# V rows of a half pass stored row first, with a newly searched order of work, in a planned two-layer kernel

## The chip, the core and the metric

The kernel runs on one core of one Trainium2 chip. The metric is device time in microseconds (us) of one execution. The engines are TensorE (PE, matrix products), VectorE (DVE), ScalarE (ACT), GpSimd (POOL) and SyncE (SP). SP and POOL issue the transfers (DMA); the transfers themselves run on 16 DMA engines. Each engine works through its own instructions in order.

## What is computed

Two layers, each an attention with a recurrent memory followed by a gated feed-forward part, on x of shape [1, 2048, 512] in bf16 (the layers use the same weights):

```python
def A(x, mem, Wq, Wk, Wv, Wo):        # 32 heads of 128, memory of 8 rows
    for s in range(64):               # segments of 32 rows
        h = concat([mem, x[s]])       # 40 rows
        q, k, v = h @ Wq, h @ Wk, h @ Wv
        p = softmax(mask(q @ k.T * scale))
        o = (p @ v) @ Wo
        mem = o[:8]                   # goes into the next segment
        out[s] = o[8:]
def B(x, w_gate, w_up, w_down):
    return (sigmoid(x @ w_gate) * (x @ w_up)) @ w_down      # 1792 wide

x = x + A(layernorm(x)); x = x + B(layernorm(x))
x = x + A(layernorm(x)); x = x + B(layernorm(x))
```

The memory rows make the 64 segments of one layer a chain. What does not depend on the memory, such as V of the x rows, can be computed ahead.

## The kernel before

**Steps.** One step (`emit_step`) does one segment of layer 0 and, six steps behind it, one segment of layer 1, so there are 70 steps; the first six and the last six have one segment alone. A step projects Q and K (L890: weights stationary, 40 or 80 columns), forms scores (L904), does the softmax on DVE and ACT (L918 to L935), transposes the probabilities (L947), multiplies by V (L973) and by Wo (L991). V of the rows that the step needs at once is made in "strips" (L815). After every four segments the feed-forward part of a block of 128 rows follows (`ffn`: L1093 gate and up, L1117 down), its weights streamed by POOL (L1085, L1086, L1111; for the last block L1040).

**V ahead of time.** V of most x rows is computed before or beside the steps and put into a scratch tensor in DRAM (`scr`, one row of 4096 values for each of 24 rows of each segment), from where each step loads its part (L859, tile `vsb`). Three routines do it. `v_pass` (matmuls at L693) takes a tile of 128 rows. `v_half` (L730) takes 64 rows: 32 are eight rows (one octet) of four segments, 32 are sixteen rows of two segments; it puts two pieces of 1024 values under each other on the 128 partitions, and its result goes out by transfers of 64 KB, 32 rows of 1024 values. `v_strip` takes 32 rows. `v_half` runs twice: once at the start of the program for block 1, and once late for the second last block of layer 1. `take_v` and `take_part` copy the normalised, transposed rows from PSUM into the tile that the matmuls read; `take_part` does the 32 columns for the sixteen rows of two segments.

**Staging at the start.** Before and during step 0 the kernel runs seven full V passes and one half pass. Their results are cast from PSUM (L1230 on ACT, L1232 on DVE) into nine staging buffers of 1024 columns, which are the tiles `wd0-2`, `wg0-2` and `wu0-2` before their use as feed-forward weights, and stored from there (L1226) by SP or POOL. A cast into a staging buffer waits until the buffer's earlier stores have landed. At the same time SP loads all of Wq, Wk, Wv and Wo (L592). Later in the program the passes use buffers `vst` and `sst`.

**Order.** Every piece of work is a `Task` with engine, duration and dependencies. `Planner.forward` lays them out in planned time, always taking the ready task that stands first in a fixed list of priorities, which the constant `SEQUENCE` holds in packed form (found by a search outside the kernel). The instructions are then emitted in order of planned start. For a store, the plan counts `nb` bytes on a modelled bus and at least `lat` ns until the buffer is free. Where the plan leaves PE idle for more than 250 ns with little work around it, `warm` puts in filler matmuls on a zero tile (`hot`, L1216), which keep PE active and compute nothing that is used. POOL's weight loads carry a wait for the matmul that the plan has last ended before them.

Of the kernel before, what the change touches and what calls it, by code (L numbers as in the profile page):

```python
# [20 lines left out]
P = 128  # L21
MEM = 8
SEG = 32
L = MEM + SEG
LW = 2 * L
XS = 24
SCOL = 24
BLK = 4
# [3 lines left out]
def fview(base, dims):  # L32
    return bass.AP(tensor=base.tensor, offset=base.offset, ap=[tuple(base.ap[0])] + [tuple(d) for d in dims])
# [20 lines left out]
;Aht@pIrb8fB#p5?Q#$k*OKvZZTq^c3OM%bV44b=*R*ZTyW=(F)eXpo=!dnjd%&eFWe?4v9B9J-6{(d-LCut;#!E)o@XKL;|1Yh}DX~>av(XnTcNY5yDmuUNDYpk)1hbP~Icf*@B%SY3<$N!PMdC+w  # L54
TzC*H?wh$B-*Ih~y~Z^1eU45ybkQ1*)!rl+2M7#!1kA=M>_00gM+A4yerPR?|M?Mj6^>>JOVW=CEf+cd3@>&Nfi0vId6NWR);FU?#N7i-E<e}?kQ5;smk7+$yR>6M$&vA+ka>GT!8=_b4-#fP#)eF7
^yFAVNqaBx;!Z*DxPH}w4u4hwLD|Xk-(55Lk^B_BDfkRj%d!v=C<*w7SG;+fg+&T)>)vE^_U=fY&kC>YwKQIya^N!=lH>FlpJ`Jr&lF|=A)fY+g;i{E@r#X;(VDk3V2MMXacuh+Y1k_asM6Wlyelal
#hat)UmCRL92k7baU(yGZ`~C!81W~7P5Erk>AYc<Vay?}YFcMj2ofpnp$(sP&YA3~nf~n+b1fFy?|Zym`QSa144a*IfxPvGj&Q1ek!IqLN$jiF41N6_7PG1D?N__fhI#wYegIrLSdO>RI&L#ADzYcB
9Qqa8r^xHgLyr2s6(Q^~qr%E_$NJ+TpJ_bc{R>AcDm>XZ4K<5#ddGdVwMU;&cRuZ|Sp~k`OZ$e|X_~sQ@384vzE1LEOy7FI`;?xf^#@MMQ)L6bC_!Zn4S4CHx9Vjn^H}pFj3R+|IJ2mzre;noNVd$S
`{%;vED%u54cw3M^F8VWNicF9{B~XUq?7A1595()pJ)9U7U(TRXvIYfie-lrSI2C)aZ1BBh3$_bQ;!I-B=8ScYh1ck&O!bB=K^(6{|r6Qx~A%7Guq$r@Iax)(DGfYMGmfWTtN`TiNx0^a_h-)zaQ;Y
Bg~_fxFI1YgW5VrkU}+v(OG0q+i!<|tAlPcRfvDusTf+wG<zAh-6L;+Y1?sI#2|g1{X&hwViH*}otG=?Uzck!7(XzcfK!b2s0y$`SNOr$pn;5(vR*N@6t6GIu9c&BiE<wNN?P(QqaXRd3M2ScK!LD`  # L60
7NE8fpYJ@UG|VxPeYSAG0la_&djDUlCG|bBoZOzAT#$(zHi(qOLpXAuXb5%<ke>jX1k1`o2(mU?ngq;3!G;hMQLm2&9MTEUYd^USvXFM#vQ$cKmjg>LrQvGCuN0;hmD;jcN{gk}oA#{rr~t7er6x;>
4TAPsm6b5FLH-g|Nf9h4giYb{D&c`|4)4`L+JTg9TM;~}=IotkUY(*Y!dPX~EqzNqLnvA&8*(y?XY|Ec+`KUE@_SSE)gkFi<&UF6JtvvpbP{*<I0G^z6$#&pA}^v95^Q4FK#<`jp&L`QSey9`{hytp
ep4|DPRnnzJfR5<$bbinu=f`jwczBNxe3uhZ<*z*5#J~4a?5s>6axJof)V}FxLuSWLQ`X$p%|GAo3ni>PtV+JzEAC$o%TiCe#d7B$K5bY%WL%|Y?`a4x@DA(YsP8dw{qC8hys!6@G=TJ3;?U)VFlx0
p<M<>KJllT(z)CRu8?`e3^R_R7%q?S32qi7rh98c7=(LFh!0=aD^hH1fNfXqg+Sja7$z4P_WGLKlHYlxk!E{x!eD5T8C@MZ?8P+s8nOs}&1S4ol`b-NnC>Xi=go6~%Yjg-4mHO!zq-ODIoX(~$HahI
@>xN0b)~I`DIDj5VKMa;CZ!v*mkbmOJ)#~W9x(W_v;<nswK`+PTq}ipg*!qKSltnE+$xw7Xt>R@wAQgZ(cg;enc1@7fR_`9(15bKuOa8wjwP|W7E?oWno808^?XT*fvZ96JauH_vO6Tmg0YAX{%<GP
x&vaN_I%f%_>nw(eGPl2kX+vA>jgyX^`O19337j8ctxfD{|+Geiw9%@3fRrZv?20mB-ZcAf?E$T01iSEPFlGkD*OepKVV{in{2e29t=mMTqiEZTBE&ID`7X6Mk+WhT~yUj_1`*B0!BsL3UYqo?S%Vq
U~wE&tp6ZiVbg<Vu#-btWwj?J)D@CYb1QP&m*#PL94pnFvBWYRVkl3T5;SG{PpgL>Y&7Ql1a;Xg%4O>TI04XhhFijc@Xaj9&%wm+O^!e2Is7ho@U?|Mv)s#Z>S-JQQ#^hP6vJ~o=FQdi%0==QiO4>}
e22-8{8_Hk?+)?_0!^US$Hin*eL}LmU1~LxfMwEBA4T-2y4BQI`Q`64rb)aYczym_%e@Wk1AuUFK%C=ysBJZCRbO!Y(YYGT<zd6Mwt&h>Ca^n2NDBRxQWx&kPPPClqibM>xRMi&j62;fUA|z^Rcv5p
F-MNEhkhZ`GG5|d;IIVWX3i~0UVC9j1JR_k)g}?mU=2&5>*Rm+{_7pfxv?)^BxJ;D;a}CKd+}lN*i{g!Cy29Nm6fs_s@A?29$S^C=sV2}7Gf8_q&p!Q-YYz<B<R6Q_L7&#1<{@t2|<x!)7#Viogyj%
#-k9m4_)fkps3Y)zWP9b))iXN6jc_5mj%JnzCGR%<`NT61>o}26adbxHKRWL;eGC_dPO$_0O%g3i&ylcjeO4Kp62wN^0l#G6AFX@sZ^p&lw_s>8|c<!RV%n$fDjRZ^Xo3)dI6V@-wLB+#PD@hFC|K{  # L70
hmxDVz+rV(-EotTD{>}bC$E+{l9$s&EXe`8-@_@{(5~Q9mF~S=mCXo-n@iGREv|B+hO}uaWNVIcBn--!6`yjXIwzk;tw$!|KNqC$<@Mh~wq+c2tXd(#Sr5!A-C=djQjW|zR>pY8ZsJpuHW?k&Vb2JQ
uK|mZtO+LXNgAg_(QsnAn`7TMhXkU87ogepo>y~+Q6YK~1|}aZxCTk*_)GF*LQIhh36&7b>}*Sf3aF_c%*8+#IpW86KlVU=PpvHDgCV0ph`o{zROB--HMhg)Z{yqq7Md>tmspIb4I7+>36}snbBa~p
2aq{FMm-sS@IOYq2mBa3IjrPDLfH_wb!L?PC1T|kd4ugY$iW8dl9Wn@+q#mR|8AO(pY8)gqHT0JZH)K^N=vOt<7^u-*$(l~x1U$PlUtaJALTr+N%)sKo=X09?|my^)5C^3SE4k&!$P)9kk;k6_2g=+
Xo<ZissDeGX{x7oi<<eTlp~=irUE^K35dz<U*p)9mm+d=#S6VL#4*xk?AUu>i@32H9Xk7!kk_K%&o5%^Sg@sug$7E7OfE13qWWUI<gX~Ww=Ovk<b`gMnA(LF)GbK-eGV(1eZq-0q2A1%j71R50jC+4
(YzP{LgPu!joT@AK^rRGm+vVYvgOLUd8rkU;M*n6fXUc#<4{U(<*Jw%^s|AolsW{O5e?q{R_5NdEk8h+662I+)Aqfs4y9uUn};G(N@<LuFs|^cT2FPBk6;o7V$@9XgP@*E$knBwHr>Rl>{fn#3`Kt?
yh8LxMxizaxtE9ijw|3QBSBOL8_*nr`Ija$bn=z6WE8x*$~+<;`&N15!cf9T9fLAG-W%WU!ZwOoz+`YmAGo$BFvfAhCU$wVm+!7~hqUD?_Qj=5pJZxrj>B%sT+T>^Mpe?7D7;6#U{20sx38&r-oZv<
@f;0J3*rnK+>gY7iHrU98Tc!cU$yG52J(53IMpe}CyZMp-M}xnkjatQP^<S=pQKx;v4)WilNu5`<Za2;cEYv!A-^%SNfLQcZHw<TrO#PTqr1ut(uD2lWlxw84HtnVFYJyK21!>3Pf#x4_<auBIOT|n
+@;+PE;I~5c;iLu7VSwLd!<@@giENcHgyQSL;-J2%c`n1>tw)5Bs}veFA<rH!^3m=l`VY}Nszs5V--R@?57p?P(+>mj+CH3TAIxks-M;?YeONKMhQ_kw+?5>kTJHu|7yVyF>aFUs;2k$08rksLjZ&}
Rec5D4v+VLqz!LXr1aXx264-a^;D{bA9Zt}4bb>Bb_oPv)r^`d2*V&n2Ps(kqh|OKVk6^jP`eI67p;O+<c~o`+;F|9sQaL-_ZCgX_3J6psL~YuH;xzf`)FU$t#f-U$eq7GKrs6{7FHkpW}34-RKFM*
9&x(UP}Ft7D%r_qN6h*20^EO0T}Wm?E1yp5ENr4Ju^T6EzeEMp)Bxm$T|rJ-CxTow#WGfD?k-in)T%Z8GRC)%u=eaRl_Ei`LMbFvL;YDLA~vt~$m$JHk6jxGBe&YFI+>Nh?*OuRiCPnCt@Nm2(HxK7  # L80
#&3kRM`t_Q;5~4|e>TMT4t<3*yUdt-xWMmna~NN*hW^#KJ3(n?D%%4`{Q+jJuR0q4-_lBy1j+FBqmip{O6sP`{bVE4hNzX|>QS_7B!LY(zVBx%^%(gHKijzO7Ss7Y(G2Y2VQ+E`6%mA5j&X?^I+)=|
P<db;>vgq@xzey}P_~g3{N0R$zl8UO=BM~MHCS_OrtXQ46onh0Y#OYaL!ZE2hoY+*G}tq}KBV|{#L!ZpbzLAaT=ge(F?IDIVMCq|mJBTHQ7CK5JO9=<=;)u%Yj;dLVc$R@gieZ`3AQh;6$rQ@iQZ@=
V>RB0haCzv329qrPHxI7KHybS8kD}@tey_pdZ+S3^+1!Zd_u(#@Bwc51(75!RI^zH@e*z62rR(bpoRk@rSm4S)S>3R3(Wmz*PCj{K$|na6?y2wU-w!(O%p6C9;oB8ZWV&<g-`Z^=HY<$y{^Z}jzCH3
UV$HD&VAwr6NtQ=vm`Xi+b-%FeG1g-5T&0ujXOTbNIQ{--zb|ZXytJtlj%7Tc{m1gKrfa#1X|V|As@F`7PH^zsG86&KLMk?>yZwc_JoAGr4WCLyeG~q5GD-oSX}2SSUvbPtzotDQV0E)5@I+Lha>C&
DS}ZGSn^mAJ`rlJm$5wePawoBajMO_l>j@?a2^U6_XSpq6S=J&H%kq4yvh*XzCIoZEU5NZczw6pMsmG}ABT=!bK@{MoQf~)lh)A0R22|G2BZt657mYk*_Tox-<g_09hV%;nL)YWonN|3AoDDx&1bL#
na*q83IB<G*_XVk%zy^teDZs~klOgm%HrUN2`M2h$pxj`RxaLf?mzW9jL{u4b|2D$NCMsLEnv^EJh#UKVL&G@cccOKTX~vm=xXk>U(k{q><I@&qD4ep%cxk8wmbLK%on{EPuT3?KiL3BsfB_s1}bzk
4k|w0K9P#^uUS|!0xaU$hu;r;-r3W&(`9`69^o6k9MDHHCCOPN>8OGEB7kEu=OXx}z3lSM@#1-PR{12eGz$@r>xDR@OeAgi{t+wvo>a0$WAP0PR9xFiZje_>iXPbTL!I&>UXu+LdY@e1wZR>E17rZB
_+1n?x+n@BHD(xyH5M3>DojQSVA(+cjxuKoi`As`(3r341mYa=<Gnp#T0tV^_cl4vhHpPKWj~AM*68j?JL({AjU)?K8UBd2%9vf(4s6E?TZ5#2(31QOu_voI?SmO95M~gstN^S&ygMVMa+7$!j~~*w
>n0u^sTKie_itwQlu@d`$Zj>onhtI!b0vvzI)BHLoRI$U?9LZM)w3v7pp8=Wpl7T(#6V4<Yi}9FIZDO+1savChV`Bwh!a{l%y(g|5;5s7w^124BDWWQHs3LPqOE<c0yvy1C^1zPbcI>H>xn!)3D3@R
0ejF8VuC8mkDGEa&ISH)g{aX_*WmOWBZF4(w=N*V^Q|3g%A^g5GeDl>1C_i%H2H#=*lDDJa2^QLXVdUf&jgBJXyA@u?p3@x%H%c$e0#Fu<fvQcuJ;TBqCnx9iYc^$QG7^^dbn&AkGoUyANwJZSqPhK  # L90
Ac>4^b;;ty(xTHUj2Jk&pY&#O3PT@VMEmFVd&dixCF6K<_$liKg3Cj*V%4jhO3@Wv#1C|H^oLjrm!TiSpn57#u77vrsh{=&Bkb^MTE8UmD`d-2n0-lFoX^MDTotFvOL_g{o`^VVLKK*p6%^F6_vHwy
L%E;$n_9PyS)iahe;p1n{}jFulI{!Q1ducj@Bbp282b;W9E58@b2ydomxZm{=_sh)pl*hMxqO1J>PY^+m4UKxeO8+f+8jLgrYvd@;1y27j3(5TF_=J=u{nd(<XyYI*}vjdwexVPNW<`~(nxQV`Q3bm
?-oKCugIcU$CVRPsibT<&C{`K8rw`m={?5dMI#P67pVd5XXX!^kt#O7jdXHtpC<=aQ_M-IF1c$;XZ^`K2CoLbmqR$Ivq{#PQJlH<ka(UMG@!Wy?g!OE;NF9YA=d6(hACy`S2&ca19}PpzuBXTH08Tu
@Lz?f1zQpJ>%+nhM7NU7yh@DH3;cUaFfmvXqEpg)AVAQFNWD5-cvZBj8C+?m#N=#2Gz`(7O!lBeMK#0m|1R1c7XDoN+Wi~qW$PQ}4iTimXzlVCmsLkEz@waJu_xEIADt!`c|AG5*imf6#OId*7Omc%
qaSm5>$72OwOoYELPh^-&@7Cs=@8jZsTMRf!amf|sTUxf>V*{4CGsTvibsUK&XTPA+hHsZ3PI1D<FlDN+@A@t933*jJ1!OX*s2Pp$90mq4+}v0yg#t*hCdVr+krL5Y2j14j40Fk8#jZ7N*okytgprx
RoHXPQ>sp|qSDHq>3xvdg;+6VhrdRa&E_m8?%9AM0TPy1JQMu{){ovpB9COdT^_c<EN`3f$n$c_`mRbTrd}lj^xn?M>P}XdptxnwQf0TIqV&^G9k3bqu^`cP>6-h=l3S1LvjFU*kOXblPG4e&Z--0E
+KhA|kTn<6k|h`R`SZ$l@Oss%2G~13Q-M0VSk1Z`OA9`BGJ=fH_Oc3Xv<Fj}eMi@iZ>m!MW2RF5Y@NbA;&M@_i@z@lO}~Tk2qmy$XZgEXy*xS3zgC_1$wK@jWjKs|ETZb2|0cV;KeBM8Uew32FhHk<
g2?JK%8cPAmwQ$OY6r?+a;<v(-M7Hlwh@ahq}H<85-$X?@JSbXE2?g5?(sr-a(*h{<wT>lJ=Q#V6#SmiIfE3+i=WW-Uc3Bi+M*W2C~08AQAXzaep+y0(7sVh)!;#B2t36^j}s4`QIIT`gP<(b<y}U;
# [361 lines left out]
class Kern:  # L460
# [222 lines left out]
    def v_pass(self, tile, keys, pieces, boot=False):  # L683

        nc, pl, DC = self.nc, self.pl, self.DC
        w = 2 if boot else 1
# [609 lines left out]
```

## Time and profile before

| | us |
|---|---|
| median of 4 runs | 1788.21 |
| lowest, highest run | 1786.0, 1788.65 |
| the profiled execution | 1786.84 |
| span of the profiled execution | 1785.1 |
| PE busy in it | 1755.4 |
| DVE, ACT, POOL busy | 1142.9, 1164.7, 575.4 |
| filler matmuls (L1216) | 103 pieces |

The span runs from the first to the last instruction of the profile; the profiled execution's own time is 1.7 us more. Matmuls are pipelined: a PE row of the timeline gives the start of its first and the modelled end of its last matmul, so neighbouring rows overlap by about 0.17 us. The mean granted clock of PE is 0.999 of full speed. The waits in the profile are inferred from semaphores; a wait for several things is put down to the one that came last.

### The profile page before, as it was taken

Reading aid. Unit: us, or ns where it says so; the run is one execution under the profiler, and the core shown is the slowest. Engines: PE = TensorE matmul, PEld = TensorE weight load, DVE = VectorE, ACT = ScalarE, POOL = GpSimd, SP = SyncE. Lnnn points to the kernel's source line nnn. Section 1 sums busy time; section 2 is a strip of 40 time slices with the busy share of each in tenths; the row PEclk is TensorE's granted clock in tenths of the full one; section 3 lists DMA queues with packets and bytes.
Section 4 is the critical chain, followed back from the end, with each engine's and each line's share of the span. In section 5 each row is a group of like instructions: output and inputs, shape, how many; then the busy total and the mean of one; then the engine's idle time right before and its main releaser. Section 6 shows DMA issues by size and latency. Waiting matters only on the chain.

```text
span 1785.1 us, 91985 instructions
## 1 busy us (share of the span) xinstructions
PE 1755.4 (98%) x39870; PEld 1518.1 (85%) x40077; DVE 1142.9 (64%) x3944; ACT 1164.7 (65%) x2960; POOL 575.4 (32%) x827
## 2 busy tenths in 40 slices
PE   9999999999999999999999999999999999999998
PEld 4588888988898898889888898988888888989886
DVE  4366566776667567656666676657656765666665
ACT  5666656666666667666766666666666666667564
POOL 4314031413333242323324231333324232333332
PEclk9999999999999999999999999999999999999999
DMA  9825254635555464455546453555555354555543
GB/s 320 278 77 150 74 154 121 182 106 153 162 156 155 135 175 124 137 150 165 158 127 202 133 154 106 161 161 165 157 148 171 110 146 139 158 155 147 157 142 94
DMA packets 138599, 270.66 MB, mean 152 GB/s; under 512 B 32954, under 2 KB 71746, under 8 KB 138194
## 3 DMA queue, kind: packets, MB, share of 16 engines
q0 software_dynamic: 56624, 181.91, 34.6%
q1 hardware_dynamic: 81570, 82.86, 16.4%
q8 instruction: 314, 5.14, 1.2%
q14 instruction: 91, 0.75, 0.1%
HBM read 220.41 MB, written 25.69 MB: 138 GB/s over the span
## 4 chain that ended last, share of the span: by engine, by line
PE 89%; DVE 5%; issue 2%; ACT 1%; DMA 1%; POOL 1%; SPq 0%; ACTq 0%; DVEq 0%; POOLq 0%
PE bank L890 31%; PE bank L991 16%; PE bank L1093 10%; PE bank L693 8%; PE bank L815 7%; PE bank L973 4%; PE bank L904 4%; PE bank L1117 4%; PE bank L947 2%; DVE st L918 1%; PE bank L1216 1%; PE bank L662 1%; DMA wg<-in_B_w_gate_dram 1%; DVE small L930 1%; DVE st L925 1%
## 5 line engine op out<-in xcount | busy, mean ns | idle before, releaser
L890 PE MATMUL bank<-hT,wk_sb 128*128 128x80 bf16 (+1 forms) x8960 | 621.6, 198 | 1.2 <-issue 1.2
L890 PE MATMUL bank<-hT,wq_sb 128*128 128x80 bf16 (+1 forms) x8960 | 622.0, 198 | 0.6
L1230 ACT CAST qku<-bank 128x480 bf16<-128x480 f32 (+3 forms) x770 | 387.9, 512 | 221.4 <-PE bank L890 139.5
L890 PEld LDWEIGHTS <-wq_sb 128*128 128x128 bf16 x8960 | 454.4, 99 | 34.1 <-issue 23.3
L890 PEld LDWEIGHTS <-wk_sb 128*128 128x128 bf16 x8960 | 450.7, 99 | 1.4 <-issue 1.4
L918 DVE TENSOR_TENSOR st<-bank,cst 40x240 f32<-40x240 f32 (+3 forms) x768 | 278.3, 368 | 188.3 <-PE bank L904 180.0
L991 PE MATMUL bank<-otsb,wo_sb 128*128 128x80 bf16 (+1 forms) x8960 | 363.6, 198 | 1.8 <-ACT otsb L1230 0.4
L991 PEld LDWEIGHTS <-wo_sb 128*128 128x128 bf16 x8960 | 336.8, 99 | 16.3 <-issue 2.0
L1086 POOL DMA_DIRECT2D wu<-in_B_w_up_dram x217 | 164.4, 758 | 241.2 <-PE bank L1093 96.5
L1230 ACT CAST otsb<-bank 128x480 bf16<-128x480 f32 (+3 forms) x420 | 199.6, 482 | 64.7 <-PE bank L973 51.7
L1085 POOL DMA_DIRECT2D wg<-in_B_w_gate_dram x217 | 164.4, 758 | 236.5 <-PE bank L1093 93.3
L1111 POOL DMA_DIRECT2D wd<-in_B_w_down_dram x217 | 154.2, 711 | 221.7 <-PE bank L904 90.6
L928 ACT ACTIVATE st<-st 80x240 f32<-80x240 f32 (+3 forms) x420 | 159.3, 381 | 37.2 <-DVE st L925 35.0
L652 POOL TENSOR_TENSOR small<-small,cst 128x1 f32<-128x1 f32 (+1 forms) x80 | 45.2, 566 | 426.8 <-DVE small L651 426.4
L1093 PE MATMUL bank<-xnT,wg 128*128 128x128 bf16 (+2 forms) x1784 | 171.5, 218 | 1.4 <-DMA wg<-in_B_w_gate_dram 0.5
L1093 PE MATMUL bank<-xnT,wu 128*128 128x128 bf16 (+2 forms) x1784 | 171.0, 218 | 0.0
L930 DVE TENSOR_REDUCE small<-st 80x6 f32<-80x240 f32 (+3 forms) x420 | 150.9, 361 | 19.5 <-ACT st L928 16.9
L904 PE MATMUL bank<-qku 128*128 128x80 bf16 (+1 forms) x2240 | 160.1, 198 | 2.0 <-DVE pb L935 0.6
L925 DVE TENSOR_TENSOR st<-st,small 80x240 f32<-80x240 f32 (+3 forms) x420 | 154.5, 369 | 3.1
L935 DVE TENSOR_TENSOR pb<-st,small 80x240 bf16<-80x240 f32 (+3 forms) x420 | 153.8, 369 | 4.0
L923 DVE TENSOR_REDUCE small<-st 80x6 f32<-80x240 f32 (+3 forms) x420 | 151.6, 362 | 4.1
L973 PE MATMUL bank<-ptsb,vsb 104*128 104x80 bf16 x2048 | 139.3, 199 | 1.8 <-ACT ptsb L1230 0.2
(103 smaller groups left out, 2343.6 us busy)
## 6 DMA issues: line engine op xcount, KB each, us to landing
wg<-in_B_w_gate_dram POOLq DMA_DIRECT2D x220, 256.0 KB, 4.3
wu<-in_B_w_up_dram POOLq DMA_DIRECT2D x220, 256.0 KB, 4.3
wd<-in_B_w_down_dram POOLq DMA_DIRECT2D x220, 256.0 KB, 4.3
vsb<-scr SPq DMA_DIRECT2D x460, 48.0 KB
vsb<-sst SPq DMA_DIRECT2D x464, 32.0 KB
scr<-vst SPq DMA_DIRECT2D x112, 96.0 KB
wv_sb<-in_A_Wv_dram SPq DMA_DIRECT2D x8, 512.0 KB
wq_sb<-in_A_Wq_dram SPq DMA_DIRECT2D x10, 384.0 KB
```

What stands on the lines that cost most here:

```text
L890: nc.tensor.matmul(o_ap, lhsT=W[:, c, h * P:(h + 1) * P], rhs=mv(c), start=(c == 0), stop=(c == DC - 1))
L904: nc.tensor.matmul(s_all(SB)[:, w0 + i, :], lhsT=fview(qku[:, i, 0, 0:1], [(1, P)]), rhs=qku[:, i, 1, 0:ncol], start=True, stop=True)
L918: pl.add("DVE", dve_ns(n, True), lambda gsz=gsz, hs=hs, st=st, SB=SB, pj_=pj_, npj_=npj_, mk=mk, idx=idx: nc.vector.tensor_tensor(out=st[p ...
L925: pl.add("DVE", dve_ns(n), lambda gsz=gsz, hs=hs, st=st, mx=mx: nc.vector.tensor_tensor(out=st[pr, hs], in0=st[pr, hs], in1=mx[pr, hs].uns ...
L928: pl.add("ACT", act_ns(n), lambda hs=hs, st=st: nc.scalar.activation(out=st[pr, hs], in_=st[pr, hs], func=ACTF.Exp, scale=self.scale), r=s ...
L930: pl.add("DVE", dve_ns(n), lambda hs=hs, st=st, sm=sm: nc.vector.tensor_reduce(out=sm[pr, hs], in_=st[pr, hs], axis=AX.X, op=ALU.add), r=s ...
L973: nc.tensor.matmul(fview(OB[:, o:o + 1], [(ncol, 2), (1, L)]), lhsT=self.vsb[halves[u // 8]][0:64 + L, j, (u % 8) * P:(u % 8 + 1) * P], rh ...
L991: nc.tensor.matmul(WB[:, c * ncol:(c + 1) * ncol], lhsT=self.wo[:, h, c * P:(c + 1) * P], rhs=otsb[:, hl, 0:ncol], start=(h == 0 and c == ...
L1085: pl.add("POOL", 760, lambda wg=wg, fs=fs: nc.gpsimd.dma_start(out=wg[:], in_=self.wgv[:, :, fs]), r=[("wo", self.H - 1)], w=[gk] + bt, la ...
L1086: pl.add("POOL", 760, lambda wu=wu, fs=fs: nc.gpsimd.dma_start(out=wu[:], in_=self.wuv[:, :, fs]), r=[("wo", self.H - 1)], w=[uk] + bt, la ...
L1093: nc.tensor.matmul(gu[:, 2 * i + k, 0:n], lhsT=W[:, c, i * P:(i + 1) * P], rhs=xnT[:, c, rw], start=(c == 0), stop=(c == DC - 1))
L1230: nc.scalar.copy(out=dst, in_=src)
```

## The change

Three things change together.

1. In `v_half`, the 32 rows that are sixteen rows of two segments are laid out and stored with the row first and the segment second; before, the segment came first. The outer dimension of the transfer's DRAM side goes from 2 to 16. `take_part` writes its columns in the new order. There are eight such transfers in the program, four at the start and four late.
2. The plan's figures: a store at the start holds its buffer for 5.0 us in place of 4.5 (`lat`), and the 64 KB stores of `v_half` and `v_strip` count 80,000 bytes in place of 65,536 (`nb`).
3. `SEQUENCE` is another list (104 packed lines, all different).

```diff
 SEQUENCE = r"""
-;Aht@pIrb8fB#p5?Q#$k*OKvZZTq^c3OM%bV44b=*R*ZTyW=(F)eXpo=!dnjd%&eFWe?4v9B9J-6{(d-LCut;#!E)o@XKL;|1Yh}DX~>av(XnTcNY5yDmuUNDYpk)1hbP~Icf*@B%SY3<$N!PMdC+w
...
 """
@@ v_pass
-                       lambda vs=vs, d=d, c0=c0, n=n: ("dma", d, vs[c0:c0 + BLK * n, 0:512 * w]), lat=3000.0 + 1500.0 * boot,
+                       lambda vs=vs, d=d, c0=c0, n=n: ("dma", d, vs[c0:c0 + BLK * n, 0:512 * w]), lat=3000.0 + 2000.0 * boot,
@@ take_part
-        dst = fview(tile[:, 0, c0:c0 + 1], [(P, self.DC), (n, 2), (1, n)])
+        dst = fview(tile[:, 0, c0:c0 + 1], [(P, self.DC), (1, 2), (2, n)])
@@ v_half
-                                     (32, d.rearrange("(i r) e -> i r e", i=BLK)[i16:i16 + 2, r16:r16 + 16], (r16 // 8, r16 // 8 + 1))):
+                                     (32, d.rearrange("(i r) e -> r i e", i=BLK)[r16:r16 + 16, i16:i16 + 2], (r16 // 8, r16 // 8 + 1))):
-                           lambda lo=lo, i=i, dd=dd, flat=flat: ("dma", dd, flat()[64 * i + lo:64 * i + lo + 32, :]), lat=3000.0 + 1500.0 * boot,
-                           r=[(sb, 0), (sb, 1)] + (["boot"] if boot else []), use=[sb], nb=65536,
+                           lambda lo=lo, i=i, dd=dd, flat=flat: ("dma", dd, flat()[64 * i + lo:64 * i + lo + 32, :]), lat=3000.0 + 2000.0 * boot,
+                           r=[(sb, 0), (sb, 1)] + (["boot"] if boot else []), use=[sb], nb=80000,
@@ v_strip
-                        r=[(sb, 0), (sb, 1)], w=[("vd", j, b, q8, kk) for kk in (2 * i, 2 * i + 1)], lat=3000.0, use=[sb], nb=65536)
+                        r=[(sb, 0), (sb, 1)], w=[("vd", j, b, q8, kk) for kk in (2 * i, 2 * i + 1)], lat=3000.0, use=[sb], nb=80000)
```

What the built programs show of it: apart from filler, both have the same matmuls, and the filler goes from 46,976 to 49,920 columns. PE's order differs in the first 170 us, in places between about 400 and 670, 760 and 940, and 1380 and 1740 us of the profile of before, and in the last step; elsewhere it is the same. At the start the stores are dealt anew between POOL and SP and among the nine buffers, and SP issues the x rows and the weights in another order. Some twenty copies in all change between ACT and DVE.

## The prediction on record

> **What bounds the kernel now.** I read the engine shares first, then PE's busy time in short stretches, then the chain of waits where PE stood still. One line of the page carries the first step:
>
> ```profile
> PE 1755.4 (98%) x39870; PEld 1518.1 (85%) x40077; DVE 1142.9 (64%) x3944; ACT 1164.7 (65%) x2960; POOL 575.4 (32%) x827
> ```
>
> The span is 1785.1 us and PE is idle for 29.7 us of it. PE's instruction stream is fixed except for its filler matmuls (L1216), so the time is real work + filler + idle + whatever runs at a reduced clock. A change of order can only move the last three. The 50 us stretches give where the idle lies: 1.3 in 0 to 50, 3.5 in 50 to 100, then 0.2 to 1.9 in each up to 1750, and 4.1 in the last 6 us, behind the last matmuls. Only 50 to 100 has one large piece. In steps of 2 us (columns: length, PE, PEld, DVE, ACT, POOL busy, clock, DMA share, GB/s):
>
> ```profile
> 56.00:58.00 2.00, 2.00 (x11) 0.94 (x10) 0.00 (x0) 0.00 (x0) 0.00 (x0) 1.00 1.01 356
> 58.00:60.00 2.00, 0.32 (x2) 0.04 (x1) 0.00 (x0) 0.00 (x0) 0.00 (x0) 1.00 1.02 326
> 60.00:62.00 2.00, 0.57 (x3) 0.29 (x3) 0.00 (x0) 1.20 (x3) 0.00 (x0) 1.00 1.06 344
> 62.00:64.00 2.00, 2.00 (x8) 0.73 (x6) 0.00 (x0) 2.00 (x5) 1.46 (x3) 0.59 1.03 335
> 64.00:66.00 2.00, 2.00 (x7) 0.76 (x6) 0.00 (x0) 0.94 (x3) 0.71 (x2) 0.55 1.08 345
> 66.00:68.00 2.00, 2.00 (x32) 0.81 (x34) 0.00 (x0) 1.28 (x3) 0.30 (x1) 1.00 1.07 387
> ```
>
> PE stops for 3.1 us, every compute engine with it, and for the next 4 us its granted clock is 0.55 to 0.59. PE's timeline prices the slow part, against a normal run of the same matmul:
>
> ```profile
> 43.97 4.48 PE L693 MATMUL bank<-wv_sb,xvf 128*128 128x512 bf16 x20
> 61.43 5.30 PE L693 MATMUL bank<-wv_sb,xvf 128*128 128x512 bf16 x16 [3.11 <-ACT wu L1230]
> ```
>
> The chain that ended last, and the waits in the first 100 us, name the cause:
>
> ```profile
> 52.23 0.64 SPq L1226
> 52.87 0.05 issue
> 52.92 1.63 SPq L592
> ...
> 54.65 6.04 DMA scr<-wu
> ...
> 60.80 0.59 ACT wu L1230
> 61.39 0.04 issue
> 61.43 5.30 PE bank L693 x16
> ```
>
> The wait itself (us in total, times, longest):
>
> ```profile
> ACT wu L1230 <- DMA scr<-wu: 10.6, 2, 7.0
> ```
>
> A cast into staging buffer wu (third of its ring) waits 7.0 us for the buffer's last store, which stood on SP's queue behind a weight load whose issue alone took 1.63 us; ACT is in order, so PE runs out of PSUM banks. The other wait in that 10.6 (3.6 us) cost PE nothing.
>
> **The change part by part.** The 20 matmuls from 43.97 need (4.48-0.17)/20 = 0.216 us each, where 0.17 is the overlap of the last one with what follows; the 16 after the stop should take 16 x 0.216 + 0.17 = 3.63 and took 5.30. So the stop costs 3.11 + 1.67 = **4.78 us**.
>
> *The staging reuse.* I added up the matmuls in both built orders (0.216 per 512 columns, 0.025 per 40) to place every cast and store. Before, the two tight reuses of that buffer leave 3.99 and 4.17 us of PE work between its last cast and the next; the second one has one store on POOL and one on SP. After, they leave 3.89 and 4.63, and both stores of each stand on POOL; every buffer with a store on SP is now refilled 9.7 us of work later or more. The first reuse is like the first of before, which did not stop PE. For the second: work position 46.76 was at 50.40 us on the clock in before, 3.64 later; so the last cast (position 45.78) runs at 49.4 to 50.0 and POOL issues the two stores at about 50.0 and 50.6 (0.55 each). POOL's stores landed 4.7 to 7.2 us after issue between 17 and 53 us when the queues were full (3.3 in one lull): 55.3 to 57.8. PE has work up to position 54.33 (two banks of step 0's projections, a transpose and three V banks stand behind the blocked cast, against four V banks before), about 58.1 us; a landing needs 0.7 more for the cast. The stop becomes 0 to 0.4 us: take off **4.78**.
>
> The skill's page "TensorE: Matmul & The Clock Gate" (Part 1, What's actually happening) has the clock fall after an idle window of about 3.4 us. The row shows 0.55 after 3.11 us. By the page the stop would be worth 3.1, by the row 4.8; the row decides.
>
> *Row first, segment second.* Eight stores of 64 KB change from 2x16 to 16x2 rows of 2 KB. In before the four on POOL landed in 6.1 to 7.2 us, 8x4 stores of the same size near them in 4.7 to 7.0: about 0.8 us later. But their buffers are refilled 14 us of work later, and what they write is first read in step 4; the four near the end (1598 to 1608 us) have no waiter in the trace. The copy that lays the rows out now writes every second element: one on ACT, 0.27 us for the like copy, with 0.36 us of idle behind it. I take 0; bounds -0.4 (one 0.4 us wait at the late staging buffer) and +0.2 (the copy doubling without cover).
>
> The page "DMA: Bandwidth & Descriptors" (Why a DMA increments its semaphore by 16 and not by 1) picks the largest number of engines up to 16 that divides both slowest dims, so 2 becomes 16. Another section (Issuing engines are not separate DMA queues) speaks against a gain: all queues share the 16 engines. With DMA shares of 1.01 to 1.08 in the stretches above, the one rule would bring these stores forward, the other moves no byte earlier; no run shows the new form yet.
>
> *Start of the program.* SP issues the x rows and V weights in another order, POOL puts two more memsets (0.23 each) ahead of its first small op. The filler up to the first V matmul goes from 23,936 to 23,808 columns: -0.05 us. POOL's first small ops at 6.91 and 9.09 have 1.4 us idle between them, which hides the memsets.
>
> *Steps 1 to 3.* Four V matmuls move from step 1 into step 0, and filler grows by 1,408 columns, 0.6 us. PE idles 1.05 us in 100 to 150, which the filler may replace: -0.46 to +0.6; I take **+0.5**.
>
> *Last step.* The same work between its V strips and its last transposes, with 1,536 more filler columns: 0.65 us. PE had 0.35 us of idle there (1750 to 1770), so +0.3 to +0.65; I take **+0.5**. After the transposes the chain goes by layernorm and is the same; POOL's last loads are released by the same places.
>
> ```profile
> 1750.00:1760.00 10.00, 10.00 (x328) 8.52 (x321) 6.40 (x21) 6.40 (x20) 2.06 (x4) 1.00 0.18 45
> 1760.00:1770.00 10.00, 9.65 (x229) 8.15 (x227) 6.44 (x28) 5.82 (x22) 5.25 (x7) 1.00 0.70 200
> ```
>
> *What is late next.* With PE 4.8 us earlier, Wo (first used at 80.5, where the weight load waited 0.4 us for it) is next. DMA shares of 0.94, 0.55, 0.86, 0.77, 0.75, 0.55 from 68 to 80 leave 3.2 us of free DMA time to bring its bytes forward; up to 1.6 us may be lost. SP's own hold there (73.8 to 77.2) is for a cast that moves along. I take **+0.3**.
>
> *Middle.* From about 400 to 670, 760 to 940 and 1380 to 1740 us the order differs in places, with equal work and filler. The 50 us stretches they fall in (400 to 650, 750 to 950, 1400 to 1700) have 8.0 us of PE idle; a tenth either way is 0.8. I take 0.
>
> Sum: -4.78 - 0.05 + 0.5 + 0.5 + 0.3 = **-3.5 us**. The profiled execution took 1786.84 (span 1785.1 and 1.7 around it), giving 1783.3; it lies 1.4 below the median of the runs shown, 1788.21, and I forecast against that: **1784.7**.
>
> **The rivals.** *A stop stays (1788 to 1790):* a store lands later than 7.2 us, or Q and K weights, asked for 4.8 us sooner, do; PE stops for up to 3 us again. For it: full DMA queues to 68 us. Against: the margin above, -0.4 to 2.1 us (58.1 - 0.7 - landing), and SP was waiting for casts at 66.2 to 69.2. The 4.8 goes back and +1.2 of filler and the like stays: 1789.4 at the worst.
>
> *Slower by over 0.2%:* the first reuse (position 35.7) becomes a stop too. It has 0.1 us less work than before, where ACT already waited 3.6 us; a store 1.5 us later than before, from POOL's denser row of issues, starts PE's idle, and from 3 us of it the clock falls. Its place is near 40 us, its price 3.1 + 1.67; with the second stop also kept, +4.8 + 1.2 = +6.0: 1794.
>
> *The order is better than counted:* stop gone, filler covering idle (-0.46 in steps 1 to 3), middle -0.8, no Wo loss: -4.78 - 0.05 - 0.46 + 0.3 - 0.8 = -5.8: 1782.4.
>
> *It doesn't do what it says:* the wider stores shorten nothing anybody waits for. That is part of the forecast; it costs no time.
>
> **How the numbers follow.** Forecast (1783 to 1786.6) 0.62; a stop stays 0.16; slower 0.13; better 0.09. About 0.2%, 3.6 us, is what a measurement of this kernel can tell from no change: the border is 1784.6, inside the forecast's case, which I split 0.35 faster, 0.27 same. Faster 0.44, same 0.43 (0.27 + 0.16), slower 0.13. The range reaches from 1782.0, the best case with the 0.4 us of the staging buffer, to 1789.5, the stop kept in full; it leaves out the slower case.
>
> **What would show it.** Right: no PE idle over 1 us and no clock below 0.9 between 20 and 100 us; the casts into wu wait under 4 us each; the strips of step 0 start near 62 instead of 66.7; Wo waits under 1.6 us; the last step 0.3 to 0.65 us longer. Wrong: a stop with a clock near 0.55 anywhere before 80 us, or matmuls of L890 or L991 waiting for weights.

## The result and the profile after

The changed kernel takes 1789.31 us (median of 35 runs, 1785.81 to 1792.69), the kernel before 1787.87 (54 runs, 1784.43 to 1790.67): a ratio of 1.001 with a 95% interval of 1.0005 to 1.0015. So it is 0.9 to 2.7 us slower, where 3.5 us less was forecast. The profiled execution took 1788.3, its span is 1786.5, 1.4 more than before.

The engine shares of the page say nothing of a loss: PE's busy time is what it was (1755.6 for 1755.4).

```profile
PE 1755.6 (98%) x39874; PEld 1517.4 (85%) x40085; DVE 1146.4 (64%) x3943; ACT 1166.3 (65%) x2961; POOL 573.7 (32%) x828
```

PE's idle time and clock by stretches of 2 us (columns as in the prediction; the last three are clock, DMA share, GB/s) show two places:

```profile
42.00:44.00 2.00, 1.14 (x7) 0.43 (x5) 0.00 (x0) 0.67 (x2) 0.00 (x0) 1.00 1.10 358
44.00:46.00 2.00, 1.90 (x11) 0.94 (x12) 0.00 (x0) 2.00 (x5) 0.33 (x1) 1.00 0.28 93
46.00:48.00 2.00, 1.95 (x10) 0.94 (x10) 0.77 (x2) 2.00 (x5) 1.98 (x5) 1.00 0.53 164
48.00:50.00 2.00, 2.00 (x14) 1.01 (x13) 0.41 (x1) 1.79 (x4) 2.00 (x5) 1.00 0.72 180
...
60.00:62.00 2.00, 0.23 (x1) 0.10 (x1) 0.00 (x0) 0.87 (x3) 0.00 (x0) 0.98 1.04 310
62.00:64.00 2.00, 2.00 (x6) 0.76 (x5) 0.00 (x0) 2.00 (x5) 0.49 (x1) 0.50 1.02 337
64.00:66.00 2.00, 2.00 (x7) 0.75 (x6) 0.00 (x0) 0.79 (x2) 0.58 (x2) 0.67 1.10 351
```

The stop at 60 us that was to go is there, with the slow clock behind it. The earlier place is new: PE misses 0.86 us at 43 us, and right behind it the DMA share, which was 1.10, falls to 0.28. The transfers have run dry, between stretches with shares of 1.10 (42 to 44 us) and 1.09 (50 to 52 us). PE's timeline gives the length of both stops and who ended them, the list of waits (0 to 110 us) the casts behind them:

```profile
43.97 0.38 PE L662 MATMUL bank<-cst,xn 128*128 128x128 bf16 x4 [0.86 <-ACT wu L1230]
...
61.77 5.30 PE L693 MATMUL bank<-wv_sb,xvf 128*128 128x512 bf16 x16 [2.03 <-ACT wu L1230]
```

```profile
ACT wu L1230 <- DMA scr<-wu: 12.2, 2, 6.2
```

Before, that line read 10.6 and 7.0. Both casts wait, as before, for stores of the buffer that they refill. The chain that ended last names the store of the second one:

```profile
50.97 0.59 ACT wu L1230
51.57 0.28 issue
51.85 0.54 POOL scr L1226
52.38 8.64 DMA scr<-wu
61.13 0.59 ACT wu L1230
61.77 5.30 PE bank L693 x16
```

It was issued at 52.4, not at 50.6, and took 8.64 us, not 4.7 to 7.2. Why the transfers ran dry is on SP's timeline:

```profile
36.56 3.01 SPq L592 DMA_DIRECT2D wk_sb<-in_A_Wk_dram  x2
45.41 0.56 SPq L1226 DMA_DIRECT2D scr<-wd  x1
46.01 1.37 SPq L754 DMA_DIRECT2D scr<-sst  x2
47.43 0.44 SPq L592 DMA_DIRECT2D wk_sb<-in_A_Wk_dram  x1
47.91 1.30 SPq L754 DMA_DIRECT2D scr<-sst  x2
49.26 0.45 SPq L592 DMA_DIRECT2D wk_sb<-in_A_Wk_dram  x1
```

From 39.6 to 45.4 us SP issues nothing. It stands at a store of wd, whose cast stands on ACT behind the cast that waits for wu. Four stores of `sst` that were ready (their casts ran at 33.3 to 34.7) and the next weight loads stand behind it. Before, SP stood only from 42.1 to 44.2, and the DMA share fell less:

```profile
41.71 0.35 SPq L777 DMA_DIRECT2D oxT<-in_A_x_dram  x1
44.24 0.64 SPq L1226 DMA_DIRECT2D scr<-wd  x1
```

```profile
44.00:46.00 2.00, 2.00 (x13) 0.94 (x11) 0.41 (x1) 2.00 (x6) 1.50 (x3) 1.00 0.73 241
46.00:48.00 2.00, 2.00 (x11) 0.89 (x10) 0.69 (x1) 1.63 (x4) 2.00 (x5) 1.00 0.87 284
48.00:50.00 2.00, 1.95 (x38) 1.46 (x37) 0.58 (x2) 1.15 (x3) 1.76 (x4) 1.00 0.73 158
```

POOL, which issues most of the stores here, stands behind the same casts on ACT, for 6.94 us after the change and 5.43 before. The row of after and then that of before:

```profile
45.67 0.52 POOL L1226 DMA_DIRECT2D scr<-wd  x1 [6.94 <-ACT wd L1230]
```

```profile
44.51 0.54 POOL L1226 DMA_DIRECT2D scr<-wd  x1 [5.43 <-ACT wd L1230]
```

Where the 1.4 us of span arise, by the start of the same matmuls in both profiles:

| place | before | after | difference |
|---|---|---|---|
| first V matmul (L693) | 13.55 | 13.43 | -0.12 |
| strips of step 0 (L815) | 66.66 | 67.00 | +0.34 |
| transposes of the first feed-forward part (L1061) | 138.70 | 140.52 | +1.82 |
| the same, ahead of the last step | 1748.94 | 1750.58 | +1.64 |
| last transposes (L1061) | 1769.41 | 1770.90 | +1.49 |

All of it lies in the first 140 us, most of it behind the strips of step 0; the last step gave 0.15 back. In the last step PE is busy throughout, as the windows that answer to those of before show:

```profile
1750.00:1760.00 10.00, 10.00 (x328) 8.37 (x324) 5.09 (x16) 5.18 (x14) 1.13 (x2) 1.00 0.12 30
1760.00:1770.00 10.00, 10.00 (x245) 8.35 (x243) 7.50 (x31) 7.00 (x27) 5.39 (x8) 1.00 0.67 191
```

### The profile page after: what moved, and what is told of

Same layout as the page of the kernel before. It is cut to its first block, busy times and chain, and to the rows that moved or that the text cites. A ratio compares the mean times of both kernels' runs of the same rounds, so it can differ in the third digit from the quotient of the medians.

```text
span 1786.5 us, 92001 instructions
## 1 busy us (share of the span) xinstructions
PE 1755.6 (98%) x39874; PEld 1517.4 (85%) x40085; DVE 1146.4 (64%) x3943; ACT 1166.3 (65%) x2961; POOL 573.7 (32%) x828
## 3 DMA queue, kind: packets, MB, share of 16 engines
q0 software_dynamic: 56256, 181.98, 34.7%
## 4 chain that ended last, share of the span: by engine, by line
PE 89%; DVE 5%; DMA 2%; issue 2%; ACT 1%; SPq 1%; POOL 0%; POOLq 0%; DVEq 0%; ACTq 0%
PE bank L890 31%; PE bank L991 16%; PE bank L1093 10%; PE bank L815 7%; PE bank L693 7%; PE bank L904 4%; PE bank L973 4%; PE bank L1117 4%; PE bank L947 2%; DVE st L918 1%; PE bank L662 1%; DVE small L930 1%; DMA wv_sb<-in_A_Wv_dram 1%; DVE small L923 1%; DVE st L925 1%
```

## The experiments

**The theory.** The two tight refills are not two separate stops. The first cast that waits (up to 43 us) holds ACT; SP, in order, holds at a store whose cast stands behind it on ACT; the transfers run dry; the loads and stores that follow are late, and PE pays later, at the second refill or at weights. The rivals: each wait costs what PE stands at it and no more; the row-first form is slow; the new order costs something elsewhere. The plan's figures (part 2 of the change) act only through the order and were not run apart.

The columns of the table: each ratio is to executions of the kernel before that ran beside the variant. "Free DMA" is 2 us x (1 - DMA share) added over the four windows from 44 to 52 us, nothing for shares over 1. "Stops" are PE's idle pieces over 0.5 us between 20 and 100 us, with what ended them ("at Wo's matmuls" where the profile names no transfer). The last column is the time from the first V matmul to the strips of step 0 (without a stop in it, 48.41 in the new order and 48.15 in the old).

| kernel | ratio (95% interval) | free DMA | stops | V to strips |
|---|---|---|---|---|
| before | 1 | 1.34 | 3.11 cast | 53.11 |
| after | 1.0010 (1.0005 to 1.0015) | 2.94 | 0.86 cast, 2.03 cast, 0.57 at Wo's matmuls | 53.57 |
| e1 after, old rows | 1.0006 (0.9997 to 1.0016) | 1.92 | 1.11 cast, 0.57 and 1.47 Wk | 49.82 |
| e2 after, both waits gone | 0.9976 (0.9966 to 0.9986) | 0.00 | 0.97 at Wo's matmuls | 48.41 |
| e3 after, first wait gone | 0.9977 (0.9969 to 0.9986) | 0.18 | none | 48.41 |
| e4 after, second wait gone | 1.0010 (1.0002 to 1.0019) | 2.48 | 0.64 cast, 2.83 and 2.05 Wk, 1.25 at Wo's matmuls | 49.46 |
| e5 before, new rows | 1.0006 (0.9997 to 1.0015) | 1.72 | 2.90 cast | 51.22 |
| e6 before, both waits gone | 0.9975 (0.9966 to 0.9983) | 0.20 | 0.81 Wo | 48.15 |
| e7 after, one store to POOL | 0.9995 (0.9986 to 1.0004) | 1.92 | 1.80 cast, 0.83 softmax, 1.09 Wo | 50.63 |
| e8 e3 without filler | 0.9990 (0.9981 to 0.9998) | 0.08 | 1.50 Wo | 48.41 |
| e9 after, plan's rule altered | 0.9978 (0.9967 to 0.9989) | 0.00 | 1.52 Wo | 48.41 |
| e12 before, first wait gone | 0.9975 (0.9965 to 0.9984) | 0.04 | 1.74 cast, 1.40 Wo | 50.06 |

The exchanged buffers are one line in `run` behind the plan; k is a task, the number behind it the staging buffer that its pass gets (0 to 2 wd, 3 to 5 wg, 6 to 8 wu). The instructions and their places stay.

**e1_old_rows**

```diff
-        dst = fview(tile[:, 0, c0:c0 + 1], [(P, self.DC), (1, 2), (2, n)])
+        dst = fview(tile[:, 0, c0:c0 + 1], [(P, self.DC), (n, 2), (1, n)])
-    (32, d.rearrange("(i r) e -> r i e", i=BLK)[r16:r16 + 16, i16:i16 + 2], ...
+    (32, d.rearrange("(i r) e -> i r e", i=BLK)[i16:i16 + 2, r16:r16 + 16], ...
```

> The changed kernel with the 16 x 2 rows laid out and stored segment first again; the order of all instructions stays. My theory (the time is lost at staging buffers that are refilled before their stores have landed, whatever the form of the rows): within 1 us of the changed kernel, PE stops at about 43 and 60 us stay within 0.5 us of 0.86 and 2.03. Rival (the row-first form itself is slower to land and costs the gain): 2 to 5 us faster than the changed kernel, and the stop at 60 us gone. Rival in the other sense (the form brings a gain that the order eats up): 1 to 4 us slower.

Measured: 1788.12 us; the interval of the ratio overlaps with that of the changed kernel, so the form is no measurable part of the loss. The second half of the expectation missed: in the one profile PE does not stop at 43 us and stops 1.11 instead of 2.03 at 60 us, but then 0.57 and 1.47 us at Wk. What the buffers gave, the weights took: PE is idle for 4.9 us between 20 and 100 us, for 4.7 in the profile after.

**e2_both_buffers, e3_first_only, e4_second_only**

```diff
         order = self.pl.plan()
+        [setattr(next(bf for bf in self.pl.bufs if bf.pool is self.bootp and k in bf.users), 'slot', s) for k, s in moves]
```

with `moves` of e2 ((211, 6), (191, 8), (282, 2), (292, 3), (318, 5), (330, 7), (324, 8), (312, 6)), of e3 ((211, 6), (191, 8), (282, 6), (312, 8), (361, 6)), of e4 ((282, 2), (292, 3), (318, 5), (330, 7), (324, 6), (312, 8)).

> The changed kernel with staging buffers exchanged between eight passes, so that the two casts that wait for a buffer's stores get buffers whose stores landed long before; every instruction keeps its engine and its place. My theory: both stops of PE go, 0.86 + 2.03 + 1.67 = 4.6 us less than the changed kernel, some 1784.7 against the 1789.3 of its median, less 0 to 1 us that weights of Q, K and Wo may take back. Rival (the weights, not the buffers, are the bound of this stretch): the stops come back at matmuls that wait for weights, gain under 2 us.

> The changed kernel with only the first of the two waits taken away (the cast at 43 us goes into another buffer; two buffers change places from there on, so that the later cast still waits for the same two stores). Theory of the chain (ACT's first wait holds SP behind a store, the DMA queues run dry from 44 to 49 us, loads and casts come late, and so the second stop): the DMA share from 44 to 48 us rises from 0.28 and 0.53 to over 0.8, and the second stop shrinks under 0.5 us; 3.5 to 5 us less than the changed kernel. Rival (each wait by itself: the second stores land late since the queues are full whatever came before): the second stop stays at 1.5 to 3 us and the gain is 0.5 to 1.2 us.

> The changed kernel with only the second wait taken away (the cast at 61 us and those after it get buffers in the order in which these come free; the cast at 43 us waits as before). Both theories: the stop of 2.03 us at 60 us and the slow clock behind it (1.67) go, 3.7 us less than the changed kernel at most. Theory of the chain: loads are late from the dry stretch at 44 to 48 us, so part of it, 0.5 to 1.5 us, comes back as waits for Q, K or Wo weights before 90 us. Rival (each wait by itself): 3.2 to 3.9 us less.

Measured: e2 1783.2, e3 1783.53, e4 1788.4 us, beside 1787.48 of the kernel before. e3 is the experiment that decides. It leaves the second cast waiting for the same two stores, and the second stop is gone all the same; with a ratio of 0.9977 it is 0.33% under the changed kernel (1.0010), 5.9 us. "Each wait by itself" promised 0.5 to 1.2. Its windows, where the changed kernel has shares of 0.28, 0.53 and 0.72, and the wait that is left:

```profile
44.00:46.00 2.00, 1.95 (x13) 1.05 (x13) 0.41 (x1) 1.17 (x2) 1.50 (x3) 1.00 1.09 381
46.00:48.00 2.00, 2.00 (x10) 0.91 (x10) 0.36 (x1) 1.27 (x3) 0.13 (x1) 1.00 1.10 388
48.00:50.00 2.00, 2.00 (x14) 1.01 (x12) 0.41 (x1) 1.27 (x3) 1.29 (x3) 1.00 1.02 370
```

```profile
ACT wu L1230 <- DMA scr<-wu: 3.3, 1, 3.3
```

3.5 to 5 us less was expected. The cast now waits 3.3 us instead of 6, which cost PE nothing; the two stores that it waits for landed 6.1 and 6.0 us after issue instead of 8.6 both. e4 is the counterpart: the second stop is gone too, and nothing is won, for PE then waits for Wk, in PE's timeline:

```profile
72.38 0.27 PE L890 MATMUL bank<-hT,wk_sb 128*128 128x40 bf16 x4 [2.83 <-DMA wk_sb<-in_A_Wk_dram]
74.80 0.31 PE L890 MATMUL bank<-hT,wk_sb 128*128 128x40 bf16 x4 [2.05 <-DMA wk_sb<-in_A_Wk_dram]
```

I had expected 0.5 to 1.5 us of that; it was 4.9 at Wk and 1.25 at Wo's matmuls. In the changed kernel the same matmuls start at 72.56 and 72.76 us without a wait, so up to there the second stop had hidden weights that were late as well. Why the second Wk transfer lands later still in e4 is not shown.

**e7_store_on_pool** takes SP's hold away and leaves the first wait; task 183 is the store of wd that SP issued at 45.4 us:

```diff
         order = self.pl.plan()
+        [setattr(tk, 'on', 'POOL') for tk in order if tk.idx == 183]
```

> The changed kernel with one store (of a third buffer, 16 x 4 rows) moved from SP to POOL: it is the one that SP waited with from 39.6 to 45.4 us. The cast at 43 us waits as before. If SP's hold is the link between the first wait and the second stop: the DMA share from 44 to 48 us rises from 0.28 and 0.53 to over 0.8, the waits for Wo weights before 90 us go, and the time falls by 2 us or more though PE's stop of 0.9 us at 43 us stays; the second stop falls under 1 us. Rival (the late casts are the link: their stores come 1 us late into full queues): the DMA share rises but the second stop stays at 2 us or grows, and the time changes by less than 1.5 us.

Measured: 1787.83 us, 0.15% (2.7 us) under the changed kernel by the two ratios, whose intervals just fail to meet, with the first stop even longer (1.80). SP issues stores and loads from 39.9 on; the share is 1.06 at 44 to 46 and 0.85 at 46 to 48, and PE does not stop at 60 us. So SP's hold is a link of the chain, worth about 2.7 of the 5.9 us. It is not all of it: SP then stands at its next store, from 44.8 to 50.8, POOL stands 7.87 us at a store of wd, the share falls to 0.47 and 0.72 at 48 to 52, and Wo is 1.09 us late, which I had expected to go. No run takes away POOL's hold alone, so how the other 3.2 us divide is not shown.

```profile
44.00:46.00 2.00, 0.93 (x7) 0.55 (x7) 0.00 (x0) 1.67 (x4) 0.00 (x0) 1.00 1.06 361
46.00:48.00 2.00, 1.95 (x10) 0.88 (x9) 0.00 (x0) 2.00 (x5) 1.31 (x3) 1.00 0.85 291
48.00:50.00 2.00, 2.00 (x14) 1.01 (x13) 0.68 (x2) 2.00 (x5) 2.00 (x5) 1.00 0.47 156
```

**e9_plan_rule** asks why the plan lets this happen, though the change raised its hold time of a staging buffer to 5.0 us:

```diff
-            T[bf.users[0]].acq.append(bf)
+            for u in bf.users[:1] if len(bf.pool.tiles) != 9 else [u for u in set(bf.users) if T[u].eng == ("PE",)]: T[u].acq.append(bf)
...
-                need.setdefault(id(bf.pool), []).append(bf)
+                if bf.slot is None: need.setdefault(id(bf.pool), []).append(bf)
...
-                for bf in tk.acq:
+                for bf in [bf for bf in tk.acq if bf.slot is None]:
```

> The changed kernel with one rule of its planner altered: a staging buffer is taken when the first of its two halves is laid out, whichever half that is (in the kernel as it stands it is taken at the lower-numbered half, so a pass whose upper half runs first writes into a buffer that the plan counts as taken later). The priorities stay; PE, DVE and SP keep their instructions' places, the buffers' names change, and the plan's 5.0 us now hold for every refill. If the refill of a buffer in flight is the whole cause: no cast waits over 1 us for a store, no stop of PE, DMA share over 0.8 from 44 to 48 us, and 1783.5 to 1785 where the kernel before has 1787.5 to 1789, a ratio of 0.9965 to 0.9985. Rival (something else in the new start costs as well): 0.999 or more, with waits for Q, K or Wo weights.

Measured: 1784.11 us, 0.9978; no cast waits for a store over 1 us, no stop until Wo (1.52). A pass fills its buffer in two halves. The plan takes the buffer at the half with the lower number (L261); where the priorities run the upper half first, its cast is planned into a buffer that the plan has not yet taken, and no hold time guards it. Both tight refills are of that kind, before and after. With the rule mended, the new priorities alone give what e3 gives.

**e5_rows_alone, e6_before_buffers, e12_before_first** do the same to the kernel before. The diff of e5 is that of e1 the other way round, on the kernel before; e6 and e12 have the line of e2 with other moves:

```diff
+        # e6:  moves = ((180, 4), (203, 8), (282, 2), (300, 3), (318, 6), (292, 1), (330, 8), (324, 5), (312, 4))
+        # e12: moves = ((180, 4), (203, 8), (282, 4), (324, 8))
```

> The kernel before with the row-first form alone (copy and store), its own order and figures. My theory: nobody waits for these stores soon, so no difference that can be measured, a ratio of 0.9993 to 1.0007 to the kernel before, and its stop of 3.1 us at 58 us stays within 1 us. Rival (16 rows let more engines take part, and the transfer lands sooner): the four stores on POOL land under 5 us instead of 6.1 to 7.2, and the time falls by 1 us or more.

> The kernel before, its order and its form, with staging buffers exchanged so that its two casts that wait (3.6 and 7.0 us) get buffers that are long free. My theory (the refill of a buffer whose stores are in flight costs the time, not the rest of the order): the stop of 3.11 us and the slow clock behind it (1.67) go, and the time falls by 3.5 to 4.8 us, to the level of the changed kernel with its first wait taken away (1783.5), within 1 us. Rival (the new order itself is the better one): it stays 1.5 us or more above that level, through weights that come late or a stop elsewhere. Rival in the other sense (the new order costs 1 us through its added filler): 1 to 1.5 us below that level.

> The kernel before with only the first of its two waits taken away (3.6 us at 42 us, which cost PE nothing; two buffers change places from there on, and the later cast still waits for the same two stores, one of them on SP behind a weight load). Theory of the chain: also here the first wait, through SP's hold (42.1 to 44.2 us) and the dry stretch behind it, makes much of the second stop; the stop of 3.1 us falls under 1.5 and the time by 2 to 4.8 us, with a DMA share from 44 to 50 us of over 0.9 in place of 0.73 to 0.92. Rival (in this kernel the second stop has its own cause, the store on SP behind the load): a stop of 2.5 us or more stays, and the time changes by less than 1 us.

Measured: e5 1789.75 us, no difference that can be measured, yet its rival had half of it right: the four 16-row stores on POOL landed 5.1, 5.2, 5.6 and 5.5 us after issue (under 5 was expected), 6.4, 6.1, 7.2 and 6.7 before. Three stores of the same size in 8 x 4 rows among them, whose form did not change, took 5.5, 5.8 and 5.5 for 5.6, 5.7 and 6.2. The row-first form lands sooner, and nobody waits for it. e6 took 1784.5 us, 0.9975: the old order without its waits is as good as the new one without them (0.9977), so neither order is better, and neither rival held. e12 took 1783.45 us, 0.9975. The wait that cost PE nothing in the profile before was worth the whole 4 us in the times; the stop in its one profile fell from 3.11 only to 1.74, between the two theories, and Wo is 1.40 late in it. That profile is of one of its two slowest executions (1786.0 us; the median is 1783.45).

```profile
60.18 3.61 PE L693 MATMUL bank<-wv_sb,xvf 128*128 128x512 bf16 x16 [1.74 <-ACT wg L1230]
```

**e8_no_filler**

```diff
-            fill = self.pl.warm(order)
+            fill = {k: v for k, v in self.pl.warm(order).items() if self.pl.tasks[k].start < 20000.0}
```

> The changed kernel with its first wait taken away, and without the filler matmuls behind the first 20 us (16.7 us of PE time by the trace). As I priced filler (1.0 of 1.25 us is paid): 10 to 13 us less, if the clock holds. If filler stands where PE would wait anyway: no gain, and the same time or up to 3 us more where the clock falls in the gaps; PE's idle time grows by what the filler took.

Measured: 1786.47 us, 0.9990 where e3 has 0.9977. The kernel without this filler is 0.13% (2.3 us) slower. (The 16.7 us of the expectation add up trace rows that overlap; at 0.216 us for 512 columns the 26,112 columns of filler behind the first V matmul are 11.0 us.) PE's idle time between 20 and 1770 us grows by 8.7 us, 1.5 of them at Wo. The last step (from the L1061 transposes ahead of it to those at its end) takes 22.0 us for 20.2. The windows of e3 (first) and e8 show how: PE idles for 1.8 us instead of 1.0, and its clock falls to 0.83. The mean clock on record is 0.997 to 0.999 in all eleven executions of e8 and 1.000 in all eleven of e3.

```profile
1760.00:1770.00 10.00, 9.04 (x206) 7.32 (x206) 5.53 (x23) 4.47 (x18) 5.65 (x8) 1.00 0.66 183
```

```profile
1760.00:1770.00 10.00, 8.21 (x180) 6.87 (x176) 4.99 (x22) 5.09 (x20) 4.13 (x7) 0.83 0.62 180
```

**e10_after_again, e11_before_again** are the two kernels unchanged, executed and profiled once more each.

> The changed kernel once more, for one look. How far do the stops move from execution to execution: the first profile has 0.86 us at 43 us and 2.03 at 60 us. If they are properties of the order: both within 0.5 us. If the landing of stores varies by 1 us with the queues: stops of 0 to 1.5 and 0.5 to 3.5, and where they are short, Q, K or Wo weights are waited for instead.

> The kernel before once more, for one look. Its first profile has a stop of 3.11 us and then a clock of 0.59 and 0.55; with the row-first form alone a stop of 2.90 us was followed by a clock of 1.00. If the clock falls with the length of the stop: 3.0 us or more again, and 0.5 to 0.6 behind it. If it depends on when the stop falls: a stop of about 3 us and either clock.

Measured: the changed kernel stops 1.22 us at 45 and 2.06 at 61 us (first profile 0.86 and 2.03), with 2.86 us of free DMA; the kernel before stops 3.24 (3.11), with 0.80 (1.34). So the stops belong to the orders. That e1, with the same order, had 0 and 1.11 suggests that a landing can still move by a microsecond; its row form differs too.

## Why the prediction was wrong

**The stop (-4.78): the step that failed.** "The first reuse is like the first of before, which did not stop PE." By work ahead of it that was nearly so (3.89 for 3.99 us), and PE's own loss there was small (0.86). But I priced a wait at what PE loses. Taking this one away (e3) is worth 5.9 us. Its cost was on SP and POOL: not the cast's wait, but who stands behind it on ACT, and who on SP and POOL behind that. The prediction follows such a queue for the second reuse and for SP's hold at 73.8 us, and left it out for the first. Its reading of before, "the other wait in that 10.6 (3.6 us) cost PE nothing", has the same fault: without that wait (e12) the kernel before is 0.25% faster, some 4 us. With e3 the stop's term is right: 48.41 us from V to strips for 53.11 before, 4.70 less where 4.78 was taken off. That e3's ratio of 0.9977 meets the forecast's 0.998 (1784.7 to 1788.21) is partly luck, since the terms for filler and Wo were off.

**The second reuse.** The margin, 4.63 us of work for 4.17 and both stores on POOL, was worked out from landings of 4.7 to 7.2 us and issues at 50.0 and 50.6. It is right in e3 (6.1 and 6.0) and wrong in the changed kernel, at the end of a dry stretch (issued at 51.9 and 52.4, landed 8.6 us later).

**The slower rival** (chance 0.13) had the place and the sign: the first reuse, near 40 us, with a stop. Its price was wrong: it put 3.1 + 1.67 us on PE at the first reuse; there were 0.86, and the rest came 17 us later. "A stop stays" (1788 to 1790) is what the profile looks like from 58 us on: its condition, a landing later than 7.2 us, was met by 8.6, and 1789.31 is in it. What made the landing late it did not say.

**Row first at 0**: right in the time (e1, e5). The neighbouring rows put what the landing could gain at about 0.8 us; it became 0.9 to 1.6 us shorter. The Trainium skill's "DMA: Bandwidth & Descriptors" (Why a DMA increments its semaphore by 16 and not by 1), where the number of engines follows from the slowest dims, so here 2 and then 16, has the direction that e5 shows; no run here counts the engines.

**Filler at +0.5 and +0.5**: the last step's term was mis-sized. It became 0.15 us shorter with 0.65 us more filler (20.2 to 20.3 us in all the profiles with the new order and its filler, 20.4 to 20.5 in those with the old). e8 says why: filler stands where PE would wait, and the clock falls without it. For steps 0 to 3 (strips to first feed-forward transposes) single profiles do not decide: 73.52 us after, 72.10 in e3, 73.71 in e2 (0.97 of it at Wo's matmuls) and 74.27 in e9 (1.52 at Wo), for 72.04 and 71.36 (e11) before.

**Wo at +0.3, bounds 0 to 1.6**: 0.57 in the changed kernel (the profile names no transfer as its end), none in e3, 0.81 to 1.52 in e6, e8, e9, e12. The bound held; it is the next late thing, as said.

**Middle at 0**: cannot be told. From the first feed-forward transposes to the last but two, the order of before takes 1555.5 to 1558.1 us in its five profiles (before, e5, e6, e11, e12), that of after 1554.8 to 1558.4 in its eight with filler. One profile does not carry terms under 2 us there.

Why the changed kernel is even slower than before (0.9 to 2.7 us) is not separately shown. Its dry stretch is longer (2.94 and 2.86 us for 1.34 and 0.80), which fits. All kernels of the table with 1.3 us or more of free DMA time between 44 and 52 us lie at 0.9995 to 1.0010; those with 0.2 or less lie at 0.9975 to 0.9978, save the one without filler (0.9990). Among the former, though, the ratios do not follow the free time within their intervals, and the second profile of before, with 0.80, lies between the groups.

## What to carry to other kernels

A wait is priced by the queue it stops: follow it from the waiting engine to everyone in order behind it, and to the transfers behind those, and look at the DMA share a few microseconds later. Where transfers were the bound of a stretch, time in which they ran dry came back here at a later wait of PE; taking that last wait away (e4) only moved it. And when a plan guards a resource, see at which instruction it counts it as taken.

## What the runs showed of the chip that was not expected

*The clock behind a stop.* It fell to 0.50 to 0.55 in the slowest 2 us behind stops of 3.11, 3.24, 2.03 and 2.06 us, to 0.51 behind the waits for Wk of e4 (2.83 and 2.05 us) and to 0.52 behind those of e1 (0.57 and 1.47 us, with 0.36 us of matmuls between them). It stayed at 1.00 behind one of 2.90 us (e5) and those of 1.74 and 1.80 us (e12, e7). PE's timeline of e5 beside that of the prediction, the same 16 matmuls in 3.61 and not 5.30 us:

```profile
61.42 3.61 PE L693 MATMUL bank<-wv_sb,xvf 128*128 128x512 bf16 x16 [2.90 <-ACT wu L1230]
```

So length alone does not decide, and the 1.67 us are not in every execution. The mean clock on record agrees: the kernel before has 0.999 in 66 of the 92 executions beside the variants, and the 26 with 1.000 are 1.5 to 2.4 us shorter in the mean (within each of the four groups that ran together). In e2, e3, e9 and e12 all have 1.000. The changed kernel's nine with 1.000 are not shorter than its others. The Trainium skill's "TensorE: Matmul & The Clock Gate" (Part 1, What's actually happening) calls the window in which activity is counted free-running. That would fit stops that end at the same place (61.4 us in before and e5) with either clock; no run here shows the window itself. A whole idle window of about 3.4 us was not needed here, as 2.03 us show.

*Landing times.* Stores on POOL landed 2.1 to 3.6 us after issue where the transfers were running dry (e7, 46.7 to 50.3 us, shares of 0.85 and 0.47) and 8.5 to 8.7 behind all that had been held (after, 50.3 to 52.4). The last two of these took 6.1 and 6.0 in e3, where the share had stayed at 1.02 to 1.10 from 42 to 50 us.

*Filler.* Some 11 us of matmuls that compute nothing save 2.3 us.
